# Ten V slots instead of nine in a two-problem attention kernel, with the room taken from wq's tail, sums and logarithms

## The chip, the cores and the metric

The kernel runs on one core of one Trainium2 chip. A core has five engines that each work through their own queue in order: TensorE (PE: matmuls, and PEld for the loads of the stationary operand), VectorE (DVE), ScalarE (ACT), GpSimd (POOL) and SyncE (SP). Engines meet only through semaphores; DMA transfers between DRAM and the on-chip SBUF are issued from a queue (here nearly all from SP) and signal a semaphore when they land. Matmul results go to PSUM, eight banks of 2 KB in each of 128 partitions. The metric is the device time of one execution in microseconds; medians are over several executions.

## The reference

Two independent attention problems, A and B, of the same size. In each there are 16 batches with 144 queries of width 448, 16 heads of width 256, and a cache of 512 keys and values for every batch and head. All inputs are bf16.

```python
q = (x @ wq).reshape(B, Sq, H, Dh).transpose(0, 2, 1, 3)
scores = einsum("bhqd,bhkd->bhqk", q, k_cache) * Dh ** -0.5
p = softmax(scores, axis=-1)
o = einsum("bhqk,bhkd->bhqd", p, v_cache)
out = o.transpose(0, 2, 1, 3).reshape(B, Sq, H * Dh) @ wo
```

The outputs of A and B stand side by side in one array of 16 x 144 x 896.

## The kernel before

The work is cut into 512 units U, one for each problem, batch and head. A Python loop over steps i (L1515 to L1571) adds instructions to the queues of the engines; the order in which it adds them is the order in which each engine runs them, and the waits between engines follow from which buffer version each instruction reads and writes (`reads=`, `writes=` of `S.add`). A buffer can be written again when every reader of its last version is done.

In step i TensorE runs the query product of a unit four steps ahead (`t_q`, L1132), the scores of unit i+3 (`t_s`, L1163), P times V of unit i (`t_pv`, L1219), on even i the matmul that sums the probabilities over the keys (`t_sum`, L1235, a product with ones), and some pieces of the output projection (`t_op_piece`, L1335), whose rate is fixed ahead. In most steps with a query product two batches of one head are done at once (288 columns, "pair Q"), and the next step has none.

The other engines serve these steps. ScalarE takes the exponentials of the scores from PSUM into pt_sb (two per unit, L1173), the logarithm of the sums (`t_ln`, L1243, one for two units) and exp of minus that, the reciprocals (`t_recip`, L1256). GpSimd adds the four key blocks of the probabilities: pp (L1183) adds two pairs, ps (L1188) adds the two results. VectorE adds the two halves of the partitions of that (`t_halves`, L1197), so that the sums of two units fill the upper and the lower half of one tile and one matmul serves both. It also moves the query products from PSUM to SBUF (L1145, L1146), checks the sums' range with two reduces (`t_check`, L1286) and multiplies P V by the reciprocals into the ring that the output projection reads (`t_evac_ot`, L1271).

The first 48 units (P0) are treated differently: their K is loaded as it lies and transposed on TensorE (L1083), and they make their sums one by one. K of all later units is transposed by the DMA, in waves of 16 units (some of 8) into a ring of 32 units (`t_load_k`, L1039). V comes in loads of two units, 512 KB (`t_load_v`, L1053), into NV slots. The other loads are x, transposed, into six slots of one batch each (`t_load_x`), wq in groups of heads (`t_load_wq`, L944 and L946) and wo (`t_load_wo`, L955). wq has 448 rows: three blocks of 128 partitions and a tail of 64 rows, which takes a fourth block of which half the partitions hold zeros.

The order of the loads is worked out by a planner at the end of the same function. `load_list` gives each load a due time from an estimate of the steps' clock, the step at which its buffer comes free, and an estimate of how long it takes. A loop then picks one load after another: the one that can start first, and among equals the one that is due first. V loads take their earliest step from the slots:

```python
v_lo = ring_free[n - NV] if n >= NV else s_min
```

The planned loads are then added to SP's queue at the step at which their buffer is free. SP waits in its queue for the buffer itself, and everything behind it on SP waits too.

## Time and profile before

| | |
|---|---|
| median of 9 executions | 1050.58 us (1047.59 to 1052.44) |
| the profiled execution's own time | 1048.27 us |
| its span, first to last instruction | 1046.4 us |
| busy: PE, ACT, DVE, POOL | 1031.9, 794.2, 741.5, 634.9 us |
| bytes moved by DMA | 294.10 MB, 281 GB/s over the span |

Times in the profile are microseconds from the span's start. A line names an engine, a line of the kernel, what it writes and what it reads, and then how often and how long. In the list of waits the three numbers are the time in total, how many times, and the longest. In the row of 40 digits each digit is the busy share of a fortieth of the span in tenths. The busy share of an engine alone doesn't say what the kernel waits for; TensorE is busy for 99% of the span, and its few waits are listed by what ended them.

### The profile page before, as it was taken

The numbers are of one execution on the slowest core, as the hardware profiler recorded it, in microseconds if no ns is written. First come the engines' busy times: TensorE is split into PE (matmuls) and PEld (weight loads), VectorE is DVE, ScalarE is ACT, GpSimd is POOL, SyncE is SP. The second block draws the span as 40 slices with busy tenths as digits, with TensorE's granted clock in tenths as the row PEclk, the third lists the DMA queues.
The fourth block names the chain that finished last, engine by engine and source line by source line (L and its number), as shares of the span: only waits on it lengthen the run. The fifth ranks groups of instructions, "written<-read, shape, count | busy, mean of one in ns | idle before, by whom it ended". The sixth has DMA issues, their size and how long they took to land.

```text
span 1046.4 us, 32447 instructions
## 1 busy us (share of the span) xinstructions
PE 1031.9 (99%) x12432; PEld 876.1 (84%) x12432; DVE 741.5 (71%) x2042; ACT 794.2 (76%) x2368; POOL 634.9 (61%) x1030
## 2 busy tenths in 40 slices
PE   8999999999999999999999899999999999999997
PEld 8999888888888888888788788888888888888885
DVE  6776677777677776777776567777776667777775
ACT  6877678778777877778766678787877777788785
POOL 3655556666666666666655556666666656666673
PEclk9999999999999999999999999999999999999999
DMA  9999999999999999999999999999999999999980
GB/s 325 364 358 316 292 269 293 272 275 274 310 282 308 268 250 262 284 305 294 253 287 353 280 273 291 295 272 302 276 279 261 283 269 313 261 261 282 283 257 13
DMA packets 590884, 294.10 MB, mean 281 GB/s; under 512 B 501440, under 2 KB 515904, under 8 KB 590720
## 3 DMA queue, kind: packets, MB, share of 16 engines
q1 hardware_dynamic: 590240, 291.72, 112.2%
q8 instruction: 99, 1.62, 0.6%
q14 instruction: 65, 0.53, 0.2%
q10 hardware_dynamic: 480, 0.23, 0.1%
HBM read 161.74 MB, written 4.13 MB: 159 GB/s over the span
## 4 chain that ended last, share of the span: by engine, by line
PE 93%; DMA 4%; SPq 1%; ACT 1%; DVE 1%; issue 0%; POOL 0%; ACTq 0%; DVEq 0%
PE s_ps L1163 23%; PE ot_ps L1219 23%; PE qp_ps L1132 23%; PE op_ps L1335 19%; DMA kt_sb<-in_B_k_cache_dram 2%; PE ot_ps L1235 2%; PE s_ps L1083 1%; PE qp_ps L1083 1%; DMA v_sb<-in_A_k_cache_dram 1%; DMA wq_sb<-in_B_wq_dram 1%; PE qp_ps L1335 1%; DMA v_sb<-in_B_v_cache_dram 0%; ACT rinv_sb L1256 0%; SPq L1053 0%; ACT pt_sb L1173 0%
## 5 line engine op out<-in xcount | busy, mean ns | idle before, releaser
L1183 POOL TENSOR_TENSOR pp_sb<-pt_sb 128x288 f32<-128x288 bf16 x512 | 384.1, 750 | 315.3 <-ACT pt_sb L1173 300.5
L1173 ACT ACTIVATE pt_sb<-s_ps 128x288 bf16<-128x288 f32 x1024 | 364.4, 408 | 179.2 <-PE s_ps L1163 173.0
L1271 DVE TENSOR_TENSOR ring<-ot_ps,rinv_sb 128x288 bf16<-128x288 f32 (+2 forms) x640 | 242.0, 395 | 150.5 <-ACT rinv_sb L1256 147.0
L1163 PE MATMUL s_ps<-qt_sb,kt_sb 128*128 128x144 bf16 x4096 | 340.5, 226 | 3.6 <-DMA kt_sb<-in_B_k_cache_dram 2.8
L1219 PE MATMUL ot_ps<-pt_sb,v_sb 128*128 128x144 bf16 x4096 | 340.2, 226 | 0.4 <-DMA v_sb<-in_B_v_cache_dram 0.2
L1163 PEld LDWEIGHTS s_ps<-qt_sb,kt_sb 128*128 128x128 bf16 x4096 | 287.2, 98 | 56.4 <-DVE qt_sb L1146 6.1
L1256 ACT ACTIVATE rinv_sb<-ln_sb 64x144 f32<-64x144 f32 x928 | 298.2, 321 | 24.2
L1132 PE MATMUL qp_ps<-xt_sb,wq_sb 128*128 128x288 bf16 (+1 forms) x2368 | 300.3, 270 | 2.8 <-DMA wq_sb<-in_B_wq_dram 1.6
L1335 PE MATMUL op_ps<-wo_sb,ring 128*128 128x448 bf16 x1120 | 285.9, 353 | 0.0
L1132 PEld LDWEIGHTS qp_ps<-xt_sb,wq_sb 128*128 128x128 bf16 x2368 | 210.9, 98 | 78.0 <-DVE ring L1271 2.0
L1219 PEld LDWEIGHTS ot_ps<-pt_sb,v_sb 128*128 128x128 bf16 x4096 | 274.3, 98 | 1.5 <-DMA v_sb<-in_B_v_cache_dram 0.7
L1188 POOL TENSOR_TENSOR p_sb<-pp_sb 128x144 f32<-128x144 f32 x464 | 226.7, 488 | 74.9 <-DVE ps_sb L1197 10.5
L1286 DVE TENSOR_REDUCE run_sb<-ot_ps 128x1 bf16<-128x144 f32 x560 | 146.6, 304 | 76.4 <-ACT ln_sb L1243 43.6
L1197 DVE TENSOR_TENSOR ps_sb<-p_sb 64x144 bf16<-64x144 f32 x464 | 159.1, 343 | 45.4 <-POOL p_sb L1188 31.7
L1146 DVE CAST qt_sb<-qp_ps 128x576 bf16<-128x576 f32 x216 | 162.1, 751 | 17.9 <-PE qp_ps L1132 15.5
L1335 PEld LDWEIGHTS op_ps<-wo_sb,ring 128*128 128x128 bf16 x1120 | 93.8, 98 | 20.1
L1243 ACT ACTIVATE ln_sb<-ot_ps 128x144 f32<-128x144 f32 x232 | 67.9, 293 | 32.2 <-PE ot_ps L1235 25.3
L1235 PE MATMUL ot_ps<-ps_sb,ones 128*128 128x144 bf16 x280 | 63.3, 226 | 0.0
L1145 DVE CAST qt_sb<-qp_ps 128x288 bf16<-128x288 f32 x80 | 35.9, 449 | 1.6 <-PE qp_ps L1132 1.1
L1091 ACT ACTIVATE kt_sb<-qp_ps 128x512 bf16<-128x512 bf16 x48 | 28.9, 602 | 0.9 <-PE qp_ps L1083 0.9
L1188 POOL TENSOR_TENSOR ps_sb<-pp_sb 128x144 bf16<-128x144 f32 x48 | 23.4, 488 | 6.9 <-PE ot_ps L1235 0.3
L1235 PEld LDWEIGHTS ot_ps<-ps_sb,ones 128*128 128x128 bf16 x280 | 27.4, 98 | 0.0
(37 smaller groups left out, 162.5 us busy)
## 6 DMA issues: line engine op xcount, KB each, us to landing
v_sb<-in_A_v_cache_dram SPq DMA_DIRECT2D x128, 512.0 KB, 7.6
v_sb<-in_B_v_cache_dram SPq DMA_DIRECT2D x128, 512.0 KB, 7.9
v_sb<-in_A_k_cache_dram SPq DMA_DIRECT2D x22, 512.0 KB, 10.1
out_dram<-ost_sb SPq DMA_DIRECT2D x36, 112.0 KB, 6.7
wo_sb<-in_A_wo_dram SPq DMA_DIRECT2D x8, 448.0 KB, 7.6
wo_sb<-in_B_wo_dram SPq DMA_DIRECT2D x8, 448.0 KB, 8.5
wq_sb<-in_B_wq_dram SPq DMA_DIRECT2D x4, 768.0 KB, 9.4
wq_sb<-in_A_wq_dram SPq DMA_DIRECT2D x3, 768.0 KB, 9.6
```

What stands on the lines that cost most here:

```text
L1132: ins = t.matmul(acc, lhsT=wq_sb[:, kc, c0:c0 + 128], rhs=xt_sb[:, kc, xo:xe + 1:max(xe - xo, 1), :], start=(kc == 0), stop=(kc == 3))
L1146: return v.tensor_copy(qt_sb[:, a:b + 1:b - a, :, :], qp_ps[:, :, 0:2 * SQ].rearrange("p e (u q) -> p u e q", u=2))
L1163: ins = t.matmul(s_ps[bank][:, (c % 2) * SQ:(c % 2 + 1) * SQ], lhsT=kt_sb[:, 2 * c + dc, ko:ko + 128], rhs=qt_sb[:, qsl, dc, :], start=(dc ...
L1173: return a.activation(pt_sb[:, psl, 2 * k:2 * k + 2, :].rearrange("p b q -> p (b q)"), s_ps[bank][:, 0:2 * SQ], AF.Exp, scale=DH ** -0.5)
L1183: return g.tensor_tensor(pp_sb[:, :, :], pt_sb[:, psl, 0:2, :], pt_sb[:, psl, 2:4, :], op=ALU.add)
L1188: return g.tensor_tensor(dst, pp_sb[:, 0, :], pp_sb[:, 1, :], op=ALU.add)
L1197: return v.tensor_tensor(ps_sb[p0:p0 + 64, sl, :], p2_sb[0:64, :], p2_sb[64:128, :], op=ALU.add)
L1219: ins = t.matmul(ot_ps[ob][:, dc * SQ:(dc + 1) * SQ], lhsT=v_sb[:, vsl, j, c * DH + dc * 128:c * DH + (dc + 1) * 128], rhs=pt_sb[:, sl, c, ...
L1256: return a.activation(rinv_sb[p0:p0 + 64, sl, :], ln_sb[h0:h0 + 64, :], AF.Exp, scale=-1.0)
L1271: ins = v.tensor_tensor(ring[:, 2 * h:2 * h + 2, r0:r0 + q1 - q0], ot_ps[ob][:, 0:2 * SQ].rearrange("p (c q) -> p c q", c=2)[:, :, q0:q1], ...
L1286: return v.tensor_reduce(run_sb[:, k, j:j + 1], ot_ps[ob][:, 2 * SQ:3 * SQ], axis=AX.X, op=op)
L1335: ins = t.matmul(acc[0:m, 0:D], lhsT=ring[:, c, col0:col0 + m], rhs=wo_sb[:, c, :], start=(c == op_first), stop=(c == op_last))
```

## The change

The kernel gets a tenth V slot (4 KB in each partition). Room for it is made in six places.

- wq's tail. The last 64 rows of an even head now lie in partitions 0 to 63 of wqt_sb and those of the odd head next to it in partitions 64 to 127 of the same columns. wq_sb loses its fourth block. Each load of a group of heads becomes one large transfer and two small ones; the head that is loaded alone as second has its tail with the first.
- x's tail. An odd head's tail stands in the upper partitions, so x's last 64 rows are needed there too: xu_sb holds a copy in its upper half (`t_tail_x`), with zeros in its lower half. An even head multiplies with the tail of xt_sb, whose upper half is zeroed again after each load. The copy and the zeroing are two VectorE instructions for each batch, added two or three steps before the first query product of that batch. x loads are due three steps earlier in the plan.
- ps_sb has one slot instead of two; for odd units of the first 48 a part of ost_sb is used.
- p2_sb is gone: ps writes its result into the first half of pp_sb, from where `t_halves` reads it.
- ln_sb is gone: the logarithm is written to slot 1 of rinv_sb, and the reciprocals of the even unit go to slot 0, those of the odd unit in place.
- The range check gathers 14 blocks of 20 sums instead of 10 of 28, keeps them in bf16, and the flag shares a tile with the statistics.

The planner runs with NV = 10 and orders the loads anew.

```diff
 
     LT = 4
     KW, KR = 16, 32
-    NV, NX = 9, 6
+    NV, NX = 10, 6
     KG = 8
     NNAT = 24
     assert KR % KW == 0 and NU % KW == 0 and KW % KG == 0
...
     assert X_GROUPS[-1][1] == NP * Bn and H == KW
     WQ_GROUPS = ((1, 2), (2, 4), (4, 8), (8, 12), (12, 16))
     WARM = 32
-    NQT, NPT, NPS, NRI, NOST = 11, 4, 2, 2, 2
+    NQT, NPT, NRI, NOST = 11, 4, 2, 2
     RS = 3
     RC = RS * 128
     XR, X_AT = 48, {0: -4, 1: -2}
...
 
     P0 = NNAT * UV
     NCK = P0 + (NT - P0) // 2
-    NRUN = max(n for n in range(1, 33) if NCK % n == 0)
+    NRUN = max(n for n in range(1, 21) if NCK % n == 0)
     assert P0 % KG == 0
     HALF_WAVES = (48, 64)
     cuts = {P0} | set(range(P0 // KW * KW + KW, NT, KW)) | set(range(HALF_WAVES[0], HALF_WAVES[1], KG))
...
         def ps(name, shape, dt):
             return mem.enter_context(nc.psum_tensor(name, shape, dt))
 
-        wq_sb = sb("wq_sb", [128, 4, H * DH], BF16)
+        wq_sb = sb("wq_sb", [128, 3, H * DH], BF16)
+        wqt_sb = sb("wqt_sb", [128, H // 2 * DH], BF16)
         wo_sb = sb("wo_sb", [128, NWO, D], BF16)
         ring = sb("ring", [128, NWO, RC], BF16)
         kt_sb = sb("kt_sb", [128, 8, KR * 128], BF16)
         v_sb = sb("v_sb", [128, NV, UV, 4 * DH], BF16)
         xt_sb = sb("xt_sb", [128, 4, NX, SQ], BF16)
+        xu_sb = sb("xu_sb", [128, NX, SQ], BF16)
         qt_sb = sb("qt_sb", [128, NQT, 2, SQ], BF16)
         pt_sb = sb("pt_sb", [128, NPT, 4, SQ], BF16)
         ones = sb("ones", [128, 128], BF16)
         pp_sb = sb("pp_sb", [128, 2, SQ], F32)
-        ps_sb = sb("ps_sb", [128, NPS, SQ], BF16)
+        ps_sb = sb("ps_sb", [128, SQ], BF16)
         rinv_sb = sb("rinv_sb", [128, NRI, SQ], F32)
-        p2_sb = sb("p2_sb", [128, SQ], F32)
-        ln_sb = sb("ln_sb", [128, SQ], F32)
         run_sb = sb("run_sb", [128, 2, NRUN], BF16)
-        runs_sb = sb("runs_sb", [128, 2, NCK // NRUN], F32)
+        runs_sb = sb("runs_sb", [128, 2, NCK // NRUN], BF16)
         ost_sb = sb("ost_sb", [128, NOST, D], BF16)
-        stat = sb("stat", [128, 4], F32)
-        flag_sb = sb("flag_sb", [128, 4], I32)
+        stat = sb("stat", [128, 8], F32)
+        flag_sb = stat.bitcast(I32)[:, 4:8]
         qp_ps = ps("qp_ps", [128, 2, 512], F32)
         s_ps = [ps("s_ps%d" % i, [128, 512], F32) for i in range(3)]
         ot_ps = [ps("ot_ps%d" % i, [128, 512], F32) for i in range(2)]
...
             t_load_wq(0, 0, 1, ACT)
 
             def e2(v):
-                return v.memset(wq_sb[64:128, 3, :], 0.0)
-            S.add(DVE, e2, writes=[("wqz", 0)], name="wqz")
+                return v.memset(xu_sb[0:64, :, :], 0.0)
+            S.add(DVE, e2, writes=[("xuz", 0)], name="xuz")
 
             def e3(g):
                 return g.memset(xt_sb[64:128, 3, :, :], 0.0)
...
             w = wqs[pr]
             sem = "wq%d" % (h0 // 4 if h1 != 1 and h1 != 2 else HG + h0)
 
+            p0, p1 = h0 // 2, (h1 + 1) // 2
+            tails = [] if h0 % 2 else [0, 1]
+
             def e(q):
-                q.dma_start(wq_sb[:, 0:3, cols], w[0:384, cols].rearrange("(c p) n -> p c n", p=128)).then_inc(
+                ins = q.dma_start(wq_sb[:, 0:3, cols], w[0:384, cols].rearrange("(c p) n -> p c n", p=128)).then_inc(
                     sems[sem], 16)
-                return q.dma_start(wq_sb[0:64, 3, cols], w[384:448, cols]).then_inc(sems[sem], 16)
-            S.add(eng, e, writes=[(("wq", h), pr) for h in range(h0, h1)], dma_sem=sem, n_dma=2,
-                  name="wq%d.%d" % (pr, h0))
+                for k in tails:
+                    src = w[384:448, p0 * 2 * DH:p1 * 2 * DH].rearrange("p (g e n) -> p g e n", e=2, n=DH)[:, :, k, :]
+                    dst = wqt_sb[k * 64:k * 64 + 64, p0 * DH:p1 * DH].rearrange("p (g n) -> p g n", n=DH)
+                    ins = q.dma_start(dst, src).then_inc(sems[sem], 16)
+                return ins
+            S.add(eng, e, writes=[(("wq", h), pr) for h in range(h0, h1)] + [(("wqt", p), pr) for p in range(p0, p1) if tails],
+                  dma_sem=sem, n_dma=1 + len(tails), name="wq%d.%d" % (pr, h0))
 
         def t_load_wo(pr, wg):
             c0 = wg * WOG
...
                 return a.activation(xt_sb[0:64, 3, g, :], acc[0:64, 3, :], AF.Copy)
             S.add(ACT, e2, reads=[("opp", ("x", g))], writes=[(("xt", g), g)], banks=["op"], name="exa%d" % g)
 
+        def t_tail_x(g):
+            sl = g % NX
+
+            def e1(v):
+                return v.tensor_copy(xu_sb[64:128, sl, :], xt_sb[0:64, 3, sl, :])
+            S.add(DVE, e1, reads=[(("xt", sl), g)], writes=[(("xu", sl), g)], name="xu%d" % g)
+            if g in X_AT:
+                return
+
+            def e2(v):
+                return v.memset(xt_sb[64:128, 3, sl, :], 0.0)
+            S.add(DVE, e2, reads=[(("xt", sl), g)], writes=[(("xt", sl), g)], name="xz%d" % g)
+
         def t_load_k(W):
             u0, u1 = WAVES[W]
             pr, r0 = divmod(u0, NU)
...
                     for kc in range(4):
                         c0 = h * DH + dc * 128
                         acc = qp_ps[:, dc, 0:2 * SQ] if n == 2 else qp_ps[:, 0, dc * SQ:(dc + 1) * SQ]
-                        ins = t.matmul(acc, lhsT=wq_sb[:, kc, c0:c0 + 128],
-                                       rhs=xt_sb[:, kc, xo:xe + 1:max(xe - xo, 1), :], start=(kc == 0), stop=(kc == 3))
+                        w, x = wq_sb[:, kc, c0:c0 + 128] if kc < 3 else wqt_sb[:, h // 2 * DH + dc * 128:][:, 0:128], xt_sb[:, kc]
+                        if kc == 3 and h % 2:
+                            x = xu_sb
+                        ins = t.matmul(acc, lhsT=w, rhs=x[:, xo:xe + 1:max(xe - xo, 1), :], start=(kc == 0), stop=(kc == 3))
                 return ins
-            S.add(PE, e, reads=[(("wq", h), pr), ("wqz", 0)] + [(("xt", g % NX), g) for g in gs],
+            S.add(PE, e, reads=[(("wq", h), pr), (("wqt", h // 2), pr), ("xuz", 0)] + [(("xt", g % NX), g) for g in gs] +
+                  ([(("xu", g % NX), g) for g in gs] if h % 2 else []),
                   writes=[(bk, ("q", U)) for bk in q_banks[:n]], banks=q_banks[:n], name="Q%d%s" % (U, ".2" if n == 2 else ""))
 
         def t_evac_q(U):
...
                 S.add(ACT, x, reads=[(("sp", bank), 2 * U + k)], writes=[(("pt", psl), U)], banks=["s%d" % bank],
                       name="ex%d.%d" % (U, k))
 
+        def ps_natural(U):
+            if U % 2:
+                return ost_sb[:, 1, 0:SQ], (("ost", 1), ("ps", U))
+            return ps_sb[:, :], ("ps", U)
+
         def t_presum(U):
             psl = U % NPT
-            sl = U % NPS
 
             def e1(g):
                 return g.tensor_tensor(pp_sb[:, :, :], pt_sb[:, psl, 0:2, :], pt_sb[:, psl, 2:4, :], op=ALU.add)
             S.add(POOL, e1, reads=[(("pt", psl), U)], writes=[("pp", U)], name="pp%d" % U)
-            dst, key = (ps_sb[:, sl, :], (("ps", sl), U)) if U < P0 else (p2_sb[:, :], ("p2", U))
+            dst, key = ps_natural(U) if U < P0 else (pp_sb[:, 0, :], ("pp", ("p2", U)))
 
             def e2(g):
                 return g.tensor_tensor(dst, pp_sb[:, 0, :], pp_sb[:, 1, :], op=ALU.add)
...
 
         def t_halves(U):
 
-            sl = U // 2 % NPS
             p0 = U % 2 * 64
 
             def e(v):
-                return v.tensor_tensor(ps_sb[p0:p0 + 64, sl, :], p2_sb[0:64, :], p2_sb[64:128, :], op=ALU.add)
-
-            S.add(DVE, e, reads=[("p2", U)], writes=[(("ps", sl), ("p", U // 2)), ("halves", U)], name="hv%d" % U)
+                return v.tensor_tensor(ps_sb[p0:p0 + 64, :], pp_sb[0:64, 0, :], pp_sb[64:128, 0, :], op=ALU.add)
+
+            S.add(DVE, e, reads=[("pp", ("p2", U))], writes=[("ps", ("p", U // 2)), ("halves", U)], name="hv%d" % U)
 
         def ring_cols(pr, b):
             g0 = pr * RP + b * SQ
...
         def t_sum(U):
             ob = U % 2
             if U < P0:
-                rhs, keys = ps_sb[:, U % NPS, :], [("ones", 0), (("ps", U % NPS), U)]
+                rhs, key = ps_natural(U)
+                keys = [("ones", 0), key]
             else:
-                sl = U // 2 % NPS
-                rhs, keys = ps_sb[:, sl, :], [("ones", 1), (("ps", sl), ("p", U // 2))]
+                rhs, keys = ps_sb[:, :], [("ones", 1), ("ps", ("p", U // 2))]
 
             def e(t):
                 return t.matmul(ot_ps[ob][:, 2 * SQ:3 * SQ], lhsT=ones[:, :], rhs=rhs, start=True, stop=True)
...
 
         def t_ln(U):
             ob = U % 2
-            dst, key = (rinv_sb[:, U % NRI, :], (("rinv", U % NRI), (U, 0))) if U < P0 else (ln_sb[:, :], ("ln", U))
+            sl = U % NRI if U < P0 else NRI - 1
+            dst, key = rinv_sb[:, sl, :], (("rinv", sl), (U, 0))
 
             def e(a):
                 return a.activation(dst, ot_ps[ob][:, 2 * SQ:3 * SQ], AF.Ln)
...
                     return a.activation(rinv_sb[:, sl, :], rinv_sb[:, sl, :], AF.Exp, scale=-1.0)
                 S.add(ACT, e, reads=[(("rinv", sl), (U, 0))], writes=[(("rinv", sl), U)], name="rc%d" % U)
                 return
-            h0 = U % 2 * 64
-            for p0 in (0, 64):
-                def e(a, p0=p0):
-                    return a.activation(rinv_sb[p0:p0 + 64, sl, :], ln_sb[h0:h0 + 64, :], AF.Exp, scale=-1.0)
-                S.add(ACT, e, reads=[("ln", U // 2 * 2)], writes=[(("rinv", sl), U)], name="rc%d.%d" % (U, p0))
+            if U % 2 == 0:
+                for p0 in (0, 64):
+                    def e(a, p0=p0):
+                        return a.activation(rinv_sb[p0:p0 + 64, 0, :], rinv_sb[0:64, NRI - 1, :], AF.Exp, scale=-1.0)
+                    S.add(ACT, e, reads=[(("rinv", NRI - 1), (U, 0))], writes=[(("rinv", 0), U)], name="rc%d.%d" % (U, p0))
+                return
+
+            def e(a):
+                a.activation(rinv_sb[0:64, NRI - 1, :], rinv_sb[64:128, NRI - 1, :], AF.Exp, scale=-1.0)
+                return a.activation(rinv_sb[64:128, NRI - 1, :], rinv_sb[64:128, NRI - 1, :], AF.Exp, scale=-1.0)
+            S.add(ACT, e, writes=[(("rinv", NRI - 1), U)], name="rc%d" % U)
 
         def t_evac_ot(U):
             pr, b, h = unit(U)
...
                 made.append((at(use) - MARGIN, free, took, fn, args))
 
             for XG, (g0, g1) in enumerate(X_GROUPS):
-                load(first_q[g0], (g1 - NX) * H - lq(NT) if g1 > NX else s_min, 1.3 + 0.55 * (g1 - g0), t_load_x, XG)
+                load(first_q[g0] - 3, (g1 - NX) * H - lq(NT) if g1 > NX else s_min, 1.3 + 0.55 * (g1 - g0), t_load_x, XG)
             for W, (u0, u1) in enumerate(WAVES):
                 last = u1 - 1 - KR
                 load(u0 - ls(u0), last - ls(last) + 1 if last >= 0 else s_min, K_FIX + 0.97 * (u1 - u0), t_load_k, W)
...
             u = i + LT
             if 0 <= u < P0:
                 t_tr(u, 1)
+            for g, at_q in first_q.items():
+                if (-2 + g if g in X_AT else at_q - 2 - g % 2) == i:
+                    t_tail_x(g)
             u = i
             if P0 <= u < NT and u % 2:
                 t_recip(u)
```

## The prediction

> **What bounds the kernel now.** I read the busy line first, then the waits of TensorE, then windows cut at the stalls they name, then the DMA issues.
>
> ```profile
> PE 1031.9 (99%) x12432; PEld 876.1 (84%) x12432; DVE 741.5 (71%) x2042; ACT 794.2 (76%) x2368; POOL 634.9 (61%) x1030
> ...
> DMA  9999999999999999999999999999999999999980
> ```
>
> TensorE is busy 99% of the span and, unusually, the DMA engines are at 9 until the last two slices. Two resources are full at once, so I ask what TensorE still waits for.
>
> ```profile
> PE s_ps L1163 <- DMA kt_sb<-in_B_k_cache_dram: 2.8, 1, 2.8
> PE qp_ps L1132 <- DMA wq_sb<-in_B_wq_dram: 1.6, 1, 1.6
> PE s_ps L1083 <- DMA v_sb<-in_A_k_cache_dram: 1.1, 3, 0.5
> ...
> PE ot_ps L1219 <- DMA v_sb<-in_B_v_cache_dram: 0.2, 1, 0.2
> ```
>
> The stalls that a V slot could touch are these few. Windows of busy time (PE, PEld, DVE, ACT, POOL, then granted clock, DMA share, GB/s):
>
> ```profile
> 519.80:521.60 1.80, 0.19 (x2) 0.12 (x2) 0.72 (x2) 0.00 (x0) 0.59 (x2) 1.00 1.03 341
> ...
> 595.40:598.70 3.30, 0.49 (x4) 0.08 (x3) 1.29 (x4) 0.72 (x3) 0.92 (x2) 0.94 1.30 255
> 598.70:601.60 2.90, 2.90 (x20) 2.35 (x21) 0.46 (x1) 1.46 (x4) 1.16 (x2) 0.50 1.00 333
> 601.60:860.00 258.40, 257.82 (x3003) 216.42 (x3002) 182.45 (x499) 200.29 (x600) 162.81 (x263) 1.00 1.17 281
> ...
> 1007.00:1031.00 24.00, 24.00 (x327) 21.17 (x325) 20.32 (x50) 21.93 (x66) 18.21 (x30) 1.00 0.33 118
> ```
>
> Start to start, TensorE loses 1.77 us at 519.9 (B's wq of heads 0 to 3 lands at 521.4), 2.97 at 595.5 (B's third K wave), and about 1.5 more because it runs at clock 0.50 until 601.5; then 0.4 and 0.3 at 718 and 753 for V loads. The DMA share over 1 in the long window says the queue never runs dry there; I found under 2 us without a packet in flight between 25 and 1010.
>
> ```profile
> 529.79 25.06 SPq L1039 DMA_TRANSPOSE kt_sb<-in_B_k_cache_dram  x1
> 554.89 1.60 SPq L1053 DMA_DIRECT2D v_sb<-in_B_v_cache_dram  x3
> ...
> 574.27 21.79 SPq L1039 DMA_TRANSPOSE kt_sb<-in_B_k_cache_dram  x1
> ```
>
> All loads go through SP in one order. A K wave of 16 units needs 16 to 18 us of transfers, a V load 1.34 (landing to landing); in that time no later V lands. The order decides which of them is late.
>
> **What the Trainium skill says.** "DMA: Bandwidth & Descriptors", section "Issuing engines are not separate DMA queues": all DMAs share the same 16 engines. The trace agrees: a V behind a K wave lands after it. A slot more adds no bandwidth. "TensorE: Matmul & The Clock Gate", section "Why this matters for your kernels": no idle gap of TensorE over about 3 us, or the clock falls. Agrees: after 2.97 us the clock was 0.50, after 1.77 it stayed 1.00. "SBUF — State Buffer", section "SBUF: two separate sides": a VectorE operation with two SBUF inputs and a GpSimd operation exclude each other for the whole instruction. Agrees, in the last batch:
>
> ```profile
> 1012.93 0.73 POOL L1183 TENSOR_TENSOR pp_sb<-pt_sb 128x288 f32<-128x288 bf16 x1 [0.21 <-ACT pt_sb L1173]
> ...
> 1012.95 0.88 DVE L1197 TENSOR_TENSOR ps_sb<-p_sb 64x144 bf16<-64x144 f32 x1
> ...
> 1014.42 0.30 DVE L1197 TENSOR_TENSOR ps_sb<-p_sb 64x144 bf16<-64x144 f32 x1
> ```
>
> The half sum (L1197) takes 0.30 alone and 0.88 when pp (L1183) has just started; 43 of 464 were so delayed.
>
> **The change part by part.**
>
> *The tenth slot: the order of loads.* The planner gives later V's an earlier place. Against K waves counted through both problems (k14 is B's first), one V fewer stands ahead of k7 to k9, one more ahead of k11 to k14, one fewer ahead of k15 and k16, then +1, +1, 0, +1, +2, 0, 0, -1, -1, -1, +1, +1, +1 up to k29. Moving one V past a wave shifts it by 1.34 us, and shifts that V by a wave. x loads, due three steps earlier, pass ahead of k7, k17 and k21 (0.9 to 5.9 us); those landed 7 us or more before their need: 0. Up to k14 margins in A are 1.8 us or more: 0. Then:
> - k14 and wq behind it land 1.34 later: the stall of 1.77 becomes 3.1 (+1.34). It ends near the gap after which the clock fell; I take it as not falling, and keep +1.5 for the range.
> - The V of units 266/267 now stands behind k15, landing about 558.7 against a need at 556.0 before. TensorE is already 1.34 late, so it stalls about 1.3 more (its total delay is then 2.6). The 0.2 at 559.7 goes.
> - k16 lands 1.34 earlier and is needed 2.6 later: its 2.97 and the 1.5 of slow clock go. At 602 TensorE is 2.6 - 2.97 - 1.5 = -1.9, that is 1.9 us ahead of before.
> - The stalls at 718 and 753 (0.7) go as well: -2.6.
> - Then the queue takes it back. It is full from 602 to 858 and moves the same bytes; the V of units 408/409 (V204) moves behind k24 and lands at about 841.0, where it was needed at 840.8 before. Nothing can be ahead of before at 841: +0.2 there. Later waves keep 1.4 to 1.9 us of margin.
>
> *Smaller loads of wq.* Tails of 128 KB in 2 KB rows become two of 64 KB in 512 B rows. The trace has 512 B packets at 27 to 57 ns and 2 KB ones at 84 to 144 ns, so the bytes cost about the same: 0, between -0.3 and +0.3 at 519.9 and at the start. One more issue on SP costs 0.5 us there, while the queue ahead is full. The zeroing at the start shrinks from 64x2048 to 64x432 (1.76 to some 0.42 us on VectorE), where TensorE waits for DMA and GpSimd: 0. The Q products keep their number and size.
>
> *x's tail in both halves.* 32 copies of 64x144 bf16 and 30 memsets of 64x72 words on VectorE. The casts out of PSUM give 449 ns at 288 columns and 751 at 576, thus 147 + 1.05 per column: 0.30 at most for a copy, an estimate; a memset lies between 0.085 (64x32) and 0.42 (64x432), say 0.12. They stand in steps where VectorE has about 0.8 us to spare; behind them wait the Q cast (L1146) and the half sum. x itself lands many us before in every case, so the new wait on it costs nothing. If a copy must wait for a pp it loses up to 0.73 more. What is lost before 841 is covered by the queue. After it some six batches: +0.1, bounds 0 and 6 x 0.75 = 4.5; without the DMA's cover, 30 x 0.25 = 7.5 at worst.
>
> *Sums in place.* p2 is gone: pp of the next unit writes where the half sum reads, so pp waits for it, with only the next sum (L1188) behind it on GpSimd, and the next half sum and then the sum matmul (L1235) waiting for that. Before, pp began a median 0.14 us before the end of the half sum (430 of 463 began earlier). Now the loop is pp 0.73 + 0.14 to ps + 0.49 + 0.03 + half sum 0.30 + 0.08 back = 1.77 us a unit, 3.54 a pair. A pair of units takes TensorE 3.8 to 4.2 us, which hides it (every sum keeps 0.23 us or more), but in B's last batch (1007 to 1031, no output projection, no pair Q) only 3.32. There the slack of the sum, 1.37 median, falls to -0.99: **+1.0 us**. As GpSimd is then idle during a half sum, I take 0.30 for it in all; had every second one 0.87, a pair would take 4.1 to 4.7, more than many pairs: up to +9.
>
> *One ps slot.* The half sum of an even unit waits for the sum matmul two units back; in 135 of 231 cases it started earlier, by 0.56 at most. It is delayed, but the checks and the eviction (L1271) behind it wait for that same matmul anyway, through a logarithm 0.29 and reciprocals 2 x 0.32. 0.
>
> *Logarithms in place.* The logarithm (L1243) now waits for the previous eviction. It began 0.05 to several us (median 0.74) after it, never before. 0; if evictions come 0.3 later, still under 0.3 a pair, on ScalarE with 24% idle.
>
> *Fourteen blocks instead of ten.* Eight more reduces of 0.18, spread over the run: 0.
>
> **Sum.** Profiled execution 1048.27 (span 1046.4 and 1.87 around it). At 841 +0.2, last batch +1.0, the rest 0.1: +1.3, thus 1049.5. The median is 2.3 above the profiled run (1050.58 against 1048.27), which gives **1051.8**, +0.1%.
>
> **The rivals.**
> 1. *Faster: the gain stays.* If V204 lands earlier than worked out (the transfers of a wave vary between 16 and 18.3 us, more than the 1.9 in question), the 2.6 of the B stalls are kept, and a tenth slot also absorbs the landings that make runs differ by 5 us. Less 1.1 for the rest: -1.5 to -4, about 1047.5. For it: the waits list, where the biggest entries go. Against: a queue full to 1010 with unchanged bytes. Chance 0.24.
> 2. *Slower: the GpSimd/VectorE loop becomes a bound* wherever a pair lasts less than the loop. It decides from 3.7 us a pair on (A's last batch, 3.70; B's odd batches with slack 0.5 to 0.65), with half sums or copies blocked as at 1012.95. +9 at full size, some +5 in the middle: 1054 to 1059. For it: 430 of 463. Against: 61% of GpSimd, and the half sum now meets an idle GpSimd. Chance 0.26.
> 3. *Slower: the wq stall passes 3 us* and the clock halves as at 598.7: 1.5, and 1.3 if V204 is then late too: +2.5 to +3, about 1054. Chance 0.10.
> 4. *No change*, the sum above. Chance 0.40.
>
> **How the numbers follow.** 0.2% (2.1 us) is about what a measurement of this kernel can tell from no change. Case 4 lies within it, between 1049 and 1053. Of rival 1 some 0.2 is faster by more, the rest same; of rivals 2 and 3 nearly all is slower: faster 0.21, same 0.42, slower 0.37. The range runs from 1047.0 (rival 1 nearly whole) to 1056.5 (half of rival 2), leaving out about 0.1 on each side.
>
> **What would show it.** Right: no wait for B's K in the 595 window and no clock of 0.5 there; a wq wait near 3 us at 520 and a V wait near 558; a V wait at about 841; pp idle before it put down to the half sum; half sums all near 0.30; TensorE with gaps in the last batch, about 1.0 us in all. Wrong: TensorE well under 1031 us and no V wait after 602 (rival 1), or idle time of TensorE before sums or Q casts spread over all batches (rival 2), or a window of clock 0.5 after 520 (rival 3). What would overturn it all is a wave of K that takes another time than here.

## The result and the profile after

The changed kernel is slower. Its median is 1058.37 us (10 runs, 1056.45 to 1062.69) against 1050.48 for the kernel before (31 runs); the ratio is 1.0082, with a 95% interval of 1.0068 to 1.0097, so between 7 and 10 us are lost. The prediction of 1051.8, at most 1056.5, was too low. The profiled execution took 1056.69 us, with a span of 1054.9.

From the page of the changed kernel, and from its list of waits of TensorE (total, times, longest):

```profile
PE 1035.4 (98%) x12432; PEld 875.2 (83%) x12432; DVE 721.7 (68%) x2112; ACT 794.4 (75%) x2368; POOL 624.0 (59%) x1030
```

```profile
PE s_ps L1186 <- DMA kt_sb<-in_B_k_cache_dram: 5.2, 4, 2.6
PE ot_ps L1245 <- DMA v_sb<-in_B_v_cache_dram: 1.9, 1, 1.9
...
PE qp_ps L1155 <- DMA wqt_sb<-in_B_wq_dram: 1.0, 1, 1.0
```

One wait for B's K became four, and together they are longer. The windows show where (columns as before: PE, PEld, DVE, ACT, POOL, clock, DMA share, GB/s):

```profile
556.50:558.70 2.20, 0.34 (x6) 0.15 (x4) 0.57 (x1) 0.71 (x2) 0.00 (x0) 1.00 1.02 327
597.80:599.30 1.50, 0.45 (x3) 0.01 (x2) 1.01 (x4) 0.72 (x3) 1.22 (x2) 1.00 0.94 152
631.80:633.50 1.70, 0.40 (x4) 0.12 (x3) 1.67 (x6) 0.08 (x1) 1.21 (x2) 1.00 0.84 226
755.90:758.80 2.90, 0.30 (x3) 0.02 (x1) 1.99 (x6) 0.25 (x1) 1.21 (x2) 1.00 1.25 247
758.80:762.80 4.00, 3.98 (x34) 3.56 (x35) 0.46 (x1) 2.17 (x6) 1.22 (x2) 0.58 1.06 382
...
1010.00:1039.00 29.00, 27.94 (x362) 22.98 (x360) 18.03 (x57) 24.78 (x75) 19.46 (x33) 1.00 0.26 94
```

The gap of 2.97 us at 595.5 has shrunk to 1.24 and its slow clock is gone. New are gaps at 556.5 (a V), 631.9 (B's fourth K wave, k17), and 755.9 (its eighth, k21), with a stretch of clock 0.58 behind the last, and a last batch in which TensorE is no longer full.

To add this up I laid the two traces side by side: the start of the first exponential of each unit after, less that before. The lag grows or shrinks where time goes. In all such comparisons below the kernel before stands for the one execution whose trace was kept. A gap of TensorE is counted from start to start of its matmuls, less the time of a matmul.

| units | lag at the end, us | change | what lies there |
|---|---|---|---|
| to 240 | +0.84 | +0.84 | five steps of 0.21 to 0.27, in batches of 16 units (e5 shows three of them to be copies of x's tail), less 0.24 at the start |
| to 248 | +1.23 | +0.39 | A's last batch |
| to 256 | +0.58 | -0.65 | wait for wq 1.12, before 1.77 |
| to 272 | +2.40 | +1.82 | V of units 266/267 |
| to 296 | -0.79 | -3.19 | k16: 1.24, before 2.97 and the slow clock |
| to 304 | +0.67 | +1.46 | k17 |
| to 360 | +1.04 | +0.37 | steps of 0.1 to 0.4, less the V waits of before |
| to 376 | +5.19 | +4.15 | k21: 2.77 and the slow clock |
| to 496 | +5.90 | +0.71 | steps of 0.2 to 0.3 (e5 shows the last to be a copy) |
| to 511, the last | +7.98 | +2.08 | B's last batch |

Two findings on their sources. First, SP's queue of the changed kernel around k17:

```profile
599.24 1.30 SPq L1073 DMA_DIRECT2D v_sb<-in_B_v_cache_dram  x2
600.59 8.46 SPq L988 DMA_TRANSPOSE xt_sb<-in_B_x_dram  x1
...
609.83 0.96 SPq L1073 DMA_DIRECT2D v_sb<-in_B_v_cache_dram  x2
610.84 19.80 SPq L1059 DMA_TRANSPOSE kt_sb<-in_B_k_cache_dram  x1
```

and of the kernel before:

```profile
600.03 22.42 SPq L1039 DMA_TRANSPOSE kt_sb<-in_B_k_cache_dram  x1
622.49 2.71 SPq L981 DMA_TRANSPOSE xt_sb<-in_B_x_dram  x1
```

The x load that stood behind k17 now stands ahead of it and holds SP for 8.46 us instead of 2.71. The wave is issued 10.8 us later and lands at 633.3 instead of 625.5. At k21 it is the same: x takes 9.57 us of SP, and the wave lands at 758.7 instead of 747.8. But x is not the whole of it. By the landings of the two traces, of the 7.8 us at k17 some 2.8 are x, 2.7 are two more V loads between k16 and k17, 1.2 the wave itself and 0.7 k16; and of the 10.9 at k21, 4.9 were already there when the wave before it, k20, landed.

Second, GpSimd and VectorE in B's last batch, from the timelines of the two engines:

```profile
1027.63 0.73 POOL L1210 TENSOR_TENSOR pp_sb<-pt_sb 128x288 f32<-128x288 bf16 x1 [0.48 <-DVE ps_sb L1223]
1028.44 0.49 POOL L1215 TENSOR_TENSOR pp_sb<-pp_sb 128x144 f32<-128x144 f32 x1
1029.48 0.73 POOL L1210 TENSOR_TENSOR pp_sb<-pt_sb 128x288 f32<-128x288 bf16 x1 [0.55 <-DVE ps_sb L1223]
...
1031.26 0.73 POOL L1210 TENSOR_TENSOR pp_sb<-pt_sb 128x288 f32<-128x288 bf16 x1 [0.48 <-DVE ps_sb L1223]
...
1029.03 0.30 DVE L1223 TENSOR_TENSOR ps_sb<-pp_sb 64x144 bf16<-64x144 f32 x1 [1.05 <-POOL pp_sb L1215]
```

pp waits for the half sum, which waits for the sum, which waits for pp. From one pp to the next it is 1.85 us, then 1.78: 3.63 a pair of units. In the kernel before TensorE needed 3.32.

### The profile page after: what moved, and what is told of

It is laid out like the page before. It is cut to its first block, busy times and chain, and to the rows that moved or that the text cites. A ratio compares the mean times of both kernels' runs of the same rounds, so it can differ in the third digit from the quotient of the medians.

```text
span 1054.9 us, 32294 instructions
## 1 busy us (share of the span) xinstructions
PE 1035.4 (98%) x12432; PEld 875.2 (83%) x12432; DVE 721.7 (68%) x2112; ACT 794.4 (75%) x2368; POOL 624.0 (59%) x1030
## 4 chain that ended last, share of the span: by engine, by line
PE 79%; DMA 11%; DVE 3%; POOL 2%; ACT 2%; SPq 1%; issue 1%; DVEq 0%; POOLq 0%; ACTq 0%
PE qp_ps L1155 20%; PE s_ps L1186 20%; PE ot_ps L1245 20%; PE op_ps L1368 16%; DMA kt_sb<-in_B_k_cache_dram 9%; PE ot_ps L1261 1%; POOL pp_sb L1210 1%; DMA wqt_sb<-in_A_wq_dram 1%; PE qp_ps L1103 1%; PE s_ps L1103 1%; ACT rinv_sb L1283 1%; POOL pp_sb L1215 1%; DVE ring L1304 1%; DVE ps_sb L1223 1%; PE qp_ps L1368 1%
## 5 line engine op out<-in xcount | busy, mean ns | idle before, releaser
L1210 POOL TENSOR_TENSOR pp_sb<-pt_sb 128x288 f32<-128x288 bf16 x512 | 373.1, 729 | 373.6 <-DVE ps_sb L1223 157.5
L1155 PE MATMUL qp_ps<-xt_sb,wq_sb 128*128 128x288 bf16 (+1 forms) x1776 | 268.7, 270 | 2.1 <-DMA wqt_sb<-in_B_wq_dram 1.0
L1215 POOL TENSOR_TENSOR pp_sb<-pp_sb 128x144 f32<-128x144 f32 x464 | 226.8, 489 | 36.4
L1223 DVE TENSOR_TENSOR ps_sb<-pp_sb 64x144 bf16<-64x144 f32 x464 | 141.2, 304 | 151.5 <-POOL pp_sb L1215 95.8
L1155 PEld LDWEIGHTS qp_ps<-xt_sb,wq_sb 128*128 128x128 bf16 x1776 | 160.7, 98 | 67.3 <-DVE qt_sb L1169 2.0
L1283 ACT ACTIVATE rinv_sb<-rinv_sb 64x144 f32<-64x144 f32 x464 | 149.5, 322 | 12.9
L1270 ACT ACTIVATE rinv_sb<-ot_ps 128x144 f32<-128x144 f32 x280 | 82.6, 295 | 36.2 <-PE ot_ps L1261 30.1
L1155 PE MATMUL qp_ps<-xu_sb,wqt_sb 128*128 128x288 bf16 (+1 forms) x304 | 81.2, 267 | 0.0
L1288 ACT ACTIVATE rinv_sb<-rinv_sb 64x144 f32<-64x144 f32 x232 | 74.5, 321 | 5.6
L1155 PE MATMUL qp_ps<-xt_sb,wqt_sb 128*128 128x288 bf16 (+1 forms) x288 | 78.5, 273 | 0.0
L1289 ACT ACTIVATE rinv_sb<-rinv_sb 64x144 f32<-64x144 f32 x232 | 74.1, 319 | 2.6
L1261 PE MATMUL ot_ps<-ps_sb,ones 128*128 128x144 bf16 x256 | 57.9, 226 | 0.0
```

The source lines that it names most:

```text
L1155: ins = t.matmul(acc, lhsT=w, rhs=x[:, xo:xe + 1:max(xe - xo, 1), :], start=(kc == 0), stop=(kc == 3))
L1210: return g.tensor_tensor(pp_sb[:, :, :], pt_sb[:, psl, 0:2, :], pt_sb[:, psl, 2:4, :], op=ALU.add)
L1215: return g.tensor_tensor(dst, pp_sb[:, 0, :], pp_sb[:, 1, :], op=ALU.add)
L1223: return v.tensor_tensor(ps_sb[p0:p0 + 64, :], pp_sb[0:64, 0, :], pp_sb[64:128, 0, :], op=ALU.add)
L1283: return a.activation(rinv_sb[p0:p0 + 64, 0, :], rinv_sb[0:64, NRI - 1, :], AF.Exp, scale=-1.0)
```

## The experiments

All ratios are to the kernel before on the same chip, with 95% intervals; medians of the kernel before differ by up to 3 us between chips. Single runs of one kernel spread over 5 to 13 us, so two ratios that differ by less than 0.3% are not told apart by the times. Where that is so, the traces decide or the question stays open.

**The changed kernel again (e0).**

> The changed kernel itself again, on the chip of the others, so that they are compared with it and with the kernel before there: 1056 to 1060; the K waits near 632 and 756 should be there again if x's place makes them, and move if they are chance.

Measured: 1057.55 us, ratio 1.0062 (1.0040 to 1.0083). Its trace has the same gaps: 1.83 at 558.8, 1.21 at 600.0, 1.36 at 633.9 and 2.71 at 757.6 with the slow clock behind it. Two executions agree, so these gaps belong to the program.

**x due at its old step (e1).**

```diff
-                load(first_q[g0] - 3, (g1 - NX) * H - lq(NT) if g1 > NX else s_min, 1.3 + 0.55 * (g1 - g0), t_load_x, XG)
+                load(first_q[g0], (g1 - NX) * H - lq(NT) if g1 > NX else s_min, 1.3 + 0.55 * (g1 - g0), t_load_x, XG)
```

> The changed kernel with the x loads due at their old step again (three steps later), everything else kept, so that x stands behind B's fourth and eighth K wave again instead of ahead of them. Theory (x ahead of a K wave makes the wave late: 1.46 us at 632, 2.77 and 1.65 of slow clock at 756): both waits go, 5 to 6 us less than the changed kernel, 1052 to 1054, what is left being the last batch and the copies of x's tail. Rival (the loop of GpSimd and VectorE is what costs everywhere): no change, 1058. Rival (a full queue hands any gain back): the waits turn up at other loads, 1056 to 1058.

Measured: 1056.50 us, 1.0056 (1.0035 to 1.0077). The list of TensorE's waits:

```profile
PE ot_ps L1245 <- DMA v_sb<-in_B_v_cache_dram: 4.7, 2, 2.8
PE s_ps L1186 <- DMA kt_sb<-in_B_k_cache_dram: 1.3, 1, 1.3
```

The K waits at 632 and 756 are gone, as expected: k17 lands at 628.7 and k21 at 748.1. But a gap of 2.99 us stands at 630.2, for the V of units 300/301 behind k17 and x, and the clock behind it is 0.50. The time is what the third theory expected: most of the gain goes to the next load that is late. Against the changed kernel run again (1.0062) the ratio itself is not told apart.

**x early in the kernel before (e2).** The opposite edit, in the kernel before.

```diff
-                load(first_q[g0], (g1 - NX) * H - lq(NT) if g1 > NX else s_min, 1.3 + 0.55 * (g1 - g0), t_load_x, XG)
+                load(first_q[g0] - 3, (g1 - NX) * H - lq(NT) if g1 > NX else s_min, 1.3 + 0.55 * (g1 - g0), t_load_x, XG)
```

> The kernel before with one edit: x loads due three steps earlier. Theory: x passes ahead of B's fourth and eighth K wave here too, and both come late: 3 to 5 us slower than before, 1054 to 1055. Rival (sums in place are the cause): 1050.5, no change.

Measured: 1051.92 us, 1.0027 (1.0010 to 1.0044): slower, by less than expected. k17 lands at 633.5 and k21 at 756.5, 8.0 and 8.7 us later than before, but no K wait follows, since TensorE in this execution was itself 2 us later by then (1.7 of it from the start of the trace). The waits come later, at V loads behind k22 and k23 (1.81 at 786, 1.51 at 816):

```profile
PE ot_ps L1219 <- DMA v_sb<-in_B_v_cache_dram: 3.5, 3, 1.6
```

The two edits move more than x, for the planner then orders the V loads differently too. Counted in SP's queue, 150 and 181 V loads stand ahead of k17 and k21 in the kernel before and in e1 (ten slots), 151 and 183 in the changed kernel and in e2 (nine slots). The shifts of V from k17 to k26, which the prediction put down to the tenth slot, and those at k7 to k9 come with x's earlier step. How much of a wave's lateness is x and how much these V loads was not tested apart.

**Nine slots in the changed kernel (e3).**

```diff
-    NV, NX = 10, 6
+    NV, NX = 9, 6
```

> The changed kernel with nine V slots, all that made the room kept. Theory (the slot gives and takes nothing by itself, x's place does it): 1057 to 1060, with the K waits at about 632 and 756 as in the changed kernel, and the waits of before at 520 and 595. Rival (the tenth slot's order is what made the waves late): 1052 to 1054.

Measured: 1052.76 us, 1.0044 (1.0025 to 1.0063), between the two and somewhat nearer the rival. A wait of 4.07 us at 597 for k16 delays TensorE so far that k17 (landing 633.5) and k21 (756.3) are on time: after 600 no DMA wait is left in B. A late load costs only what an earlier one has not cost already. The waits of this kernel are therefore not shares that add up. The last batch costs what it did (+2.06).

**The sum in place, alone, in the kernel before (e4).**

```diff
-            dst, key = (ps_sb[:, sl, :], (("ps", sl), U)) if U < P0 else (p2_sb[:, :], ("p2", U))
+            dst, key = (ps_sb[:, sl, :], (("ps", sl), U)) if U < P0 else (pp_sb[:, 0, :], ("pp", ("p2", U)))
...
```

> The kernel before with one edit: the sum is written into pp_sb and read from there by the half sum, p2_sb gone. Theory (the loop of pp, ps and half sum, 3.63 us a pair in the changed kernel, exceeds TensorE's pair only in the last batches of A and B, where TensorE needs 3.32 in B's): 2 to 2.5 us slower, 1052.5 to 1053. Rival (the loop binds in all batches): 1056 to 1059. As first worked out: 1.0 slower, 1051.5.

Measured: 1049.79 us, 1.0011 (0.9994 to 1.0028), not told apart from no change by the time. The trace shows the size: in B's last batch the lag grows by 1.35 us, with pairs of 3.56, in A's last by 0.1, and in other batches not at all. So the loop does not bind elsewhere. This kernel has none of the other parts of the change, and a pair is 0.07 shorter than the 3.63 of the changed kernel; which part makes the 0.07 was not tested.

Its loads stand in the order of the kernel before, yet its trace has neither the wait for wq at 520 nor the clock of 0.5 near 600, and of the 2.97 for k16 a gap of 0.86 is left:

```profile
595.40:598.70 3.30, 3.30 (x38) 2.65 (x36) 1.57 (x4) 2.10 (x8) 1.47 (x3) 1.00 1.05 385
598.70:601.60 2.90, 2.90 (x35) 2.43 (x34) 2.09 (x8) 1.95 (x6) 2.18 (x4) 1.00 1.05 400
```

B's first wave, issued at 491.0 in both, landed at 512.6 here and at 516.3 in the trace of the kernel before. Between units 248 and 304 this execution came 5.0 us ahead of that one, with no tenth slot and no new order. So the stalls that the change was to remove are not the same in every execution, and a gain of this size there says little in one trace.

**The changed kernel without later copies (e5).**

```diff
-                    t_tail_x(g)
+                    if g < NX:
+                        t_tail_x(g)
...
```

> The changed kernel without the copy of x's tail and without the zeroing after it for all batches past the first six (the upper rows of later batches are then stale: work is left out to read its time). Theory (each batch's copy of 0.19 and memset of 0.12 delay one Q cast in two batches by 0.21 to 0.25, ten times): 1.5 to 2 us less than the changed kernel, 1056 to 1057, the steps of 0.2 gone. Rival (a full queue covers them): 1058.

Measured: 1056.23 us, 1.0051 (1.0033 to 1.0068). The steps in the batches that end at units 96, 192, 224 and 480 (0.23 three times, 0.34) fall to 0.07 or 0.08, which settles what made these. The one that ends at 128 stays (0.27, here 0.31) and is something else. The time hardly follows: TensorE reaches 600 some 2 us earlier than in the changed kernel and then waits 2.00, 1.34, 2.04 and 1.63 us for K and V at 629, 753, 784 and 843.

**The sum apart in the changed kernel (e6).**

```diff
-        pp_sb = sb("pp_sb", [128, 2, SQ], F32)
+        pp_sb = sb("pp_sb", [128, 2, SQ], BF16)
+        p2_sb = sb("p2_sb", [128, SQ], F32)
-            dst, key = ps_natural(U) if U < P0 else (pp_sb[:, 0, :], ("pp", ("p2", U)))
+            dst, key = ps_natural(U) if U < P0 else (p2_sb[:, :], ("p2", U))
...
```

> The changed kernel with the sum in a tile of its own again (p2_sb), room for it made by keeping pp in bf16. Theory (loop of GpSimd and VectorE): the last batch of B goes back to 3.3 us a pair from 3.63, that of A too: 2 to 2.5 us less than the changed kernel, 1056. Rival (the other serial waits, one ps slot and the logarithm in place, set that pair): 1058.

Measured: 1053.59 us, 1.0046 (1.0033 to 1.0059). From unit 496 to the end the lag grows by 0.04 us instead of 2.08. That is the loop, shown both ways; one ps slot and the logarithm in place, which this kernel keeps, do not bind there. What the list of GpSimd's waits says of the loop in the changed kernel, and here:

```profile
POOL pp_sb L1210 <- DVE ps_sb L1223: 157.5, 263, 1.9
```

```profile
POOL pp_sb L1211 <- ACT pt_sb L1197: 303.1, 420, 11.3
```

With the sum apart pp waits for the exponentials again. The price is that half sums meet GpSimd once more: they take up to 0.879 us, as in the kernel before (0.878), where in the changed kernel none took over 0.307.

**Three things mended, ten slots (e8).** The diffs of e1 and e6, and the copies of odd batches a step later:

```diff
-                if (-2 + g if g in X_AT else at_q - 2 - g % 2) == i:
+                if (-2 + g if g in X_AT else at_q - 2) == i:
```

> The changed kernel with three things undone: x loads due at their old step, the sum apart with pp in bf16, and the copies of odd batches moved by a step into one without a Q cast. Ten slots stay. Theory (these three are all but the order of V around 557 to 600): the 8 us fall to between 0 and 2, 1049 to 1052. Rival (the slot's order of loads itself is worth 3 us of loss in any case): 1053 to 1055.

Measured: 1053.71 us, 1.0042 (1.0028 to 1.0056), as the rival expected. At unit 296 this kernel is 3.86 us ahead of the one before; at unit 304 it is 0.92 behind.

```profile
626.90:630.20 3.30, 0.35 (x7) 0.19 (x5) 1.10 (x5) 0.85 (x3) 1.44 (x3) 1.00 0.95 278
630.20:634.50 4.30, 4.30 (x32) 3.15 (x32) 1.95 (x6) 1.29 (x5) 0.46 (x1) 0.60 1.05 397
```

The V of units 300/301, first behind k17 and x, lands at 629.98; in the kernel before it landed at 630.16. TensorE came earlier, so it waited 3.11 us, and then ran at half clock. Being early was paid for twice.

**The same with nine slots (e10)**, whose loads then have the order of the kernel before.

```diff
-    NV, NX = 10, 6
+    NV, NX = 9, 6
```

> The three mended things with nine slots, whose loads then come in the order of the kernel before. What is left of the change is wq's halves, the copies of x's tail, one ps slot and the logarithm in place. Theory (these cost 0 to 1 us, the copies no more where they stand now): 1050 to 1051.5, and what lies between this and the ten slots mended, about 2 to 3 us, is the price of the planner's new order around 560 to 630. Rival (the slot's order costs nothing, the rest of the compute parts does): 1053 to 1054 as with ten.

Measured: 1050.86 us, 1.0024 (1.0005 to 1.0043), and K and V waits of 3.77 at 597, 0.72, 0.59 and 0.91. With e8 on another chip the two ratios overlap: that the tenth slot by itself costs or gives anything was not shown.

**The order of loads set by hand (e9)**, ten slots, one V more ahead of every wave from k17 on, before's number ahead of k14 to k16. The loop moves V loads across wave W in the finished plan until V_AHEAD[W] of them stand ahead; the rest is e8.

```diff
+    V_AHEAD = dict(zip(range(14, 30), (127, 134, 144, 151, 159, 167, 174, 182, 191, 198, 206, 215, 224, 232, 240, 248)))
...
+        for W in range(14, len(WAVES)):
...
```

> The three mended things and ten slots, with the plan's order changed after planning: before B's first three K waves as many V loads as in the kernel before, before every later wave one more, which is what the tenth slot has room for. Theory (a full queue sets when things land, but the V behind a wave is needed sooner than the wave): the V waits of 2 to 3 us near 557 and 627 go, the queue still holds the third and fourth wave to about 597 and 629: 1 to 3 us less than the kernel before, 1047 to 1049. Rival (the queue's total decides, the wait only moves to a K wave): equal to the kernel before, 1050.

Measured: 1050.70 us, 1.0027 (1.0010 to 1.0044). The waits near 557 and 627 are gone. At unit 344 this kernel has gained 3.2 us on the one before since unit 8, and it loses 3.5 at 751, to a V behind k21 and x (2.15) and the clock of 0.62 after it.

**One V more ahead of k21, copies on ScalarE (e12).**

```diff
-    V_AHEAD = dict(zip(range(14, 30), (127, 134, 144, 151, 159, 167, 174, 182, 191, 198, 206, 215, 224, 232, 240, 248)))
+    V_AHEAD = dict(zip(range(14, 30), (127, 134, 144, 151, 159, 167, 174, 183, 191, 198, 206, 215, 224, 232, 240, 248)))
...
+                if g not in X_AT:
+                    return v.activation(xu_sb[64:128, sl, :], xt_sb[0:64, 3, sl, :], AF.Copy)
```

The copies of odd batches stand at their own step again.

> As the last kernel with ten slots, with one V more ahead of B's eighth wave (the V of units 364/365, which was 2.15 us late behind that wave and an x load), and the copies of x's tail on ScalarE instead of VectorE. Theory (after 600 TensorE was 3.2 us ahead of the kernel before and lost it at 751 to one V and the slow clock behind it): the wait at 751 goes or falls under 1 us, the clock stays, 2 to 3 us less than the last one, 1047 to 1049, that is 0 to 2 less than the kernel before. Rival (every gain is handed back at the next load that the full queue brings late): 1050 again, with a new wait after 751.

Measured: 1048.96 us, 1.0001 (0.9984 to 1.0018): the same as the kernel before. Of TensorE's waits for DMA only A's first K loads are left (ScalarE waits 1.8 us for x, in two copies):

```profile
PE s_ps L1107 <- DMA v_sb<-in_A_k_cache_dram: 1.4, 2, 0.9
```

So with ten slots and an order of loads made for them, an execution can have no DMA wait of TensorE in B. It is 4.9 us better than that of the kernel before between units 248 and 304. But e4 gained 5.0 there with nine slots and the old order, so this is not shown to be the slot's. It loses 2.3 between units 24 and 240 and 1.3 after 304, in steps of 0.1 to 0.5. Half sums that meet GpSimd and the copies may make them; that was not tested apart.

**Sums in place but for the last batch, copies on VectorE, the same order (e13).**

```diff
+        p2_last = xu_sb[:, 2:4, :].rearrange("p a q -> p (a q)").bitcast(F32)
+        def sum_at(U):
+            if U < NT - H:
+                return pp_sb[:, 0, :], ("pp", ("p2", U)), []
+            return p2_last, ("p2", U), [(("xu", sl), "p2") for sl in (2, 3)]
...
```

> The changed kernel (sums in place, copies on VectorE where it has them) with x due at its old step, the order of loads of the last kernel, and the sums of B's last batch alone apart, in the slots of xu_sb that are free by then. Theory (the last kernel had no DMA wait left in B, but lost some 0.27 in every second batch to half sums that met a GpSimd operation, and to copies on ScalarE; in place they don't): 1 to 3 us less than the kernel before, 1047 to 1049. Rival (with TensorE earlier the queue becomes late again somewhere): equal to the kernel before, with a DMA wait of 1 us or more after 600.

Measured: 1050.87 us, 1.0022 (1.0008 to 1.0036). The time is the rival's. TensorE has no wait for DMA after 600, but one of 2.98 us at 751 for VectorE, which itself waits for a load.

```profile
753.69 0.19 DVE L1042 COPY xu_sb<-xt_sb 64x144 bf16<-64x144 bf16 x1 [3.33 <-DMA xt_sb<-in_B_x_dram]
...
753.99 0.30 DVE L1232 TENSOR_TENSOR ps_sb<-pp_sb 64x144 bf16<-64x144 f32 x1
```

The copy waits for x, which lands at 753.66 behind k21, and the half sum waits behind the copy; the sum matmul (L1270) waits for that.

**The copy a step later, behind the eviction (e14).**

```diff
-                if (-2 + g if g in X_AT else at_q - 2 - g % 2) == i:
+                if (-2 + g if g in X_AT else at_q - 1 - g % 2) == i:
                     t_tail_x(g)
...
```

The loop that adds them moves from ahead of `t_halves` to behind `t_evac_ot`.

> As the last kernel, with the copies of x's tail a step later and behind everything else of their step on VectorE (for every even batch in the step just before its first Q product, instead of two steps before it and ahead of the half sum). Theory (the copy held VectorE for 3.33 us until x had landed, and the half sum and eviction behind it made TensorE wait 2.98 at 751): that wait goes, at most 1 us of it is left as a wait of the Q product for x itself; 2 to 3 us less than the last kernel, 1047.5 to 1049, 0.5 to 2.5 less than the kernel before. Rival (with that wait gone the full queue is late with the next load): equal to the last kernel, with a DMA wait near 755.

Measured: 1077.35 us, 1.0282 (1.0254 to 1.0310), the opposite of what was expected.

```profile
PE qp_ps L1156 <- DVE xt_sb L1048: 25.8, 15, 2.8
```

The wait for x is gone, but now the Q product waits for copy and zeroing in every second batch, since VectorE comes to them 1.7 us on average after TensorE wants the next Q. Of the two places tried, the early one needs x early, and the late one costs the product.

## Why the prediction was wrong, by its steps

*x loads "pass ahead of k7, k17 and k21 (0.9 to 5.9 us); those landed 7 us or more before their need: 0".* This step failed, and it is the largest error: it put at 0 what measured 5.6 us. By its own figures x (up to 5.9) and one V (1.34) already took 7.24 of the margin of some 7.3 at k17, TensorE was forecast to come 1.9 earlier there, and two more V loads stand ahead of k21. Measured, k17 landed 7.8 us later and k21 10.9. The x load held SP for 8.46 and 9.57 us ahead of a wave, where it took 2.71 and 4.09 behind one. The step also took the shifts of V from k17 to k26 for the slot's, where e2 shows them to come with x. In the lag k17 cost 1.46, and k21 4.15, that is 2.77 of waiting and the slow clock after it: together 5.6 of the 6.0 us by which the lag grows between units 296 and 376.

*x "lands many us before in every case, so the new wait on it costs nothing".* True of the changed kernel, whose trace has no such wait. But x is early there: with x at its old step the copy held VectorE for 1.1 us in e1 and e8, and for 3.3 in e13. The two zeros were one trade, and the prediction looked at each alone.

*The order at 520 to 602.* The V of units 266/267 was predicted to land at 558.7 and did at 558.6; its wait was 2.02 (predicted 1.3). wq waited 1.12 where 3.1 was predicted: it landed at 522.0, only 0.6 later, and TensorE was itself 1.2 late through the copies and A's last batch. k16 kept a wait of 1.24 where none was predicted, because it landed at 599.2 and not 1.34 earlier. The slow clock went as predicted. In sum -0.8 at unit 296, where -1.9 was predicted. Both stand against one execution of the kernel before; against one like e4's there would have been little to win.

*"Then the queue takes it back".* Right in kind: e1, e5, e8 and e9 all came early somewhere after 590 and waited at the next late load. The figure was wrong, and so was the bound. The step put the lag at 841 at +0.2; measured it was 5.4, and V204, which landed at 844.3 and not at 841.0, found TensorE later still. Nor does the queue hold everyone to one time: e4, with the old order, passed 841 3.4 us ahead, its k24 having landed at 836.6 and not at 841.0. The prediction had named a wave of another length as what would overturn it. A full queue took gains back, and with the worse order it took more, and in nine of thirteen waits over 2.1 us TensorE paid again in clock.

*The loop in the last batch.* Right in mechanism, mis-sized: 1.0 predicted, 2.08 measured. A pair took 3.63 and not 3.54, so 0.31 over TensorE's 3.32 and not 0.22. Of the two turns of a pair one took the predicted 1.77 (1.78); in the other the half sum began 0.10 after the sum, not 0.03. That 0.07 is missing in e4, which lost 1.35; it may be the one ps slot, put at 0, but no run has that part alone. A's last batch, put under the rival, lost 0.39.

*Half sums all at 0.30.* Right: 302 to 307 ns for all 464. Rival 2, whose size of +9 comes nearest the result, is refuted in its mechanism: pp waits for half sums 263 times, but outside the last batches of A and B TensorE does not wait for it (e4).

*Copies.* 0.19 and 0.12 measured, 0.30 and 0.12 estimated. The cover named for them was right for A (about half of the 1.2 us is gone at 256), and after 841 the lag grows by 0.5 up to the last batch, where 0.1 was predicted; one of these steps e5 shows to be a copy.

After 841 the lag grows by 2.6 us, by steps that no load covers; the 5.4 before it are what the order of loads came to, with copies and A's last batch partly inside it. What stays open: how much each part is worth in the median. The intervals of e1, e3, e5, e6 and e8 overlap, and delays that a full queue covers do not add. With the three things mended and nine slots (e10) 0.24% is left, and no run shows that the tenth slot wins anything.

## What to carry to other kernels

When DMA queue and TensorE are both full, price a reordering by landing times against needs, load by load, with every transfer that passes ahead counted at its duration in that place, and don't call a margin safe that the moved loads use up. A new wait and the earlier load that serves it are one step: ask what the earlier load pushes back. Room in memory that is bought with serial steps has to be paid in the stretch with the least work per step, here the last batch.

## What the runs showed of the hardware

The clock's fall follows no bound on the length of a gap here. Of the gaps of TensorE over 1.3 us from unit 250 on in thirteen traces (all but e12, which has none, and e14), those up to 2.06 us (19 of them) left the clock at 1.00. Of the longer ones, 2.15, 2.71, 2.77, 2.85, 2.97, 2.99, 3.11, 3.77 and 4.07 us were followed by a mean clock between 0.50 and 0.71 in the next 2.5 us, but 2.27, 2.65, 2.90 and 2.98 were not. The bound of about 3 us that the prediction took from the Trainium skill ("TensorE: Matmul & The Clock Gate", section "Why this matters for your kernels") is too high as a safe one: 2.15 us was enough once.

What sorts nearly all of them is a grid in the traces. Apart from the two ends of the kernel, fifteen traces have nine slow stretches. Each lasts 3.41 us at clock 0.50, which loses up to 1.7 us, and begins a whole number of 3.41 us after the clock first became full. The share of one such 3.41 us that TensorE was busy told whether the next was slow: 0.14 to 0.32 was followed by a slow one all eight times, 0.42 once in three, 0.44 or more never. These are two of the three (e9 with its gap of 2.15, then e6 with its gap of 2.65):

```profile
750.55:753.96 3.41, 1.43 (x19) 1.16 (x18) 1.16 (x5) 1.60 (x5) 1.91 (x3) 1.00 0.85 297
753.96:757.37 3.41, 3.41 (x20) 2.48 (x19) 2.13 (x6) 1.33 (x4) 0.45 (x1) 0.50 1.05 402
```

```profile
757.80:761.21 3.41, 1.43 (x11) 0.79 (x9) 2.42 (x7) 1.15 (x4) 1.77 (x3) 1.00 1.26 256
761.21:764.63 3.42, 2.91 (x38) 2.58 (x39) 0.70 (x2) 2.27 (x7) 1.39 (x3) 1.00 1.05 386
```

The gap of 2.90 in e6 fell on two stretches, busy for 0.66 and 0.54 of them, and cost no clock. So by these traces a gap's place on the grid counts beside its length; what decides at a share of 0.42 is open.

Around k17 and k21 a transpose of x ahead of the wave held SP for 6.6 to 9.7 us (the changed kernel, e0, e2, e3, e5, e6), and behind the wave for 2.6 to 4.9 (the others), though in the changed kernel and the one before it landed 1.9 to 3.4 us after the transfer before it in both places. What SP waits for while it holds is not shown. The first V behind x landed 2.2 and 3.9 us after it in the changed kernel, where the V loads between k20 and x stand 1.3 to 2.8 apart.
